# One batch of block-sparse attention written as a list of single steps, with wider block sums, no score bias and fewer unread matmuls

## The chip, the cores and the metric

The kernel runs on one core of one Trainium2 chip. The metric is the device time of one execution in microseconds (us). The span that the profile prints is about 1.8 us shorter than this time, from the first to the last instruction.

## The reference

Four batches of attention, 8 heads, 768 positions, 64 wide. Each query sees the 31 keys nearest to it and one summary per block of 32 keys (the maximum of the keys, the mean of the values). A gated feed-forward layer follows: 3072 tokens, width 512, inner width 1536.

```python
k_sum = k.reshape(B, H, nb, 32, D).max(axis=3)
v_sum = v.reshape(B, H, nb, 32, D).mean(axis=3)
mask_l = np.abs(pos[:, None] - pos[None, :]) < 16
scores_s = scale * einsum('bhsd,bhnd->bhsn', q, k_sum) + np.log(32)
a = softmax(concatenate([where(mask_l, scale * q @ k.T, -1e9), scores_s]))
x = a @ concatenate([v, v_sum])          # per head, then heads side by side
out = (sigmoid(x @ w_gate) * (x @ w_val)) @ w_out
```

## The kernel before

TensorE (PE) is the queue that everything stands in. The heads are taken in four pairs. Batch 0 is special: nothing can hide behind a feed-forward layer that has not begun. So its first half (384 queries) goes through a hand-made list. The second half is spread between the first feed-forward units (a unit is four `gp` and four `vp` matmuls for 128 of the 1536 inner columns), and batches 1 to 3 are spread over the rest. Five pieces matter here.

The keep-busy matmul: it multiplies a tile of ones, and nobody reads the result.

```python
def warm(self, out, n):
    for _ in range(n):
        nc.tensor.matmul(out=out, lhsT=blank, rhs=blank[:, 0:out.shape[-1]], start=True, stop=True)
```

The scores of a pair's first half. The window mask comes in as a matmul that first writes -30720 into the score tile wherever a key is out of reach; the scores are then added on top.

```python
def S1(self, p, step, fill=0):
    if step:
        self.warm(self.fill, fill)
    if step == 0:
        ...
        for i in range(2):
            nc.tensor.matmul(out=self.sc[0:W, i, 0:HALF], lhsT=ident[0:W, 0:W],
                             rhs=bias.rearrange("p t w -> p (t w)"), start=True, stop=False, ...)
        return
    # step 1: 12 small matmuls, start=False; step 2: 2 for the far keys, then exp
```

Block sums of the values, one pair at a time, 26 matmuls of 64 columns in two column groups of the array; and the far part of the weighted sum, 12 matmuls of 64-column weights.

```python
def sums(self, p, fill=0, vsp=None):
    ...
    for t in range(NQ + 1):
        for i in range(2):
            nc.tensor.matmul(out=vsp[64 + 32 * i:96 + 32 * i, 0:64], lhsT=zband[0:64, 30 - 2 * t:62 - 2 * t],
                             rhs=self.vx[0:64, NQ * (2 * p + i) + t, 0:64], ...)

def far(self, p):
    for t in range(6):
        for i in range(2):
            nc.tensor.matmul(out=av[64 * (t % 2):64 * (t % 2) + 64, t // 2, i, 0:64],
                             lhsT=self.P[p][96:120, i, t, :], rhs=vs[96:120, 2 * p + i, :], ...)
```

And the list itself, whose numbers are counts of unread matmuls:

```python
wait(36)
...
a0.T1(0)              # transposes of the keys of pair 0
wait(14)
a0.T2(0, "dve")       # transposes of its queries
a0.S1(0, 0); a0.T1(1); a0.T2(1, "dve"); a0.S1(0, 1); a0.T1(2); a0.S1(0, 2)
a0.S1(1, 0, 6); a0.S1(1, 1); a0.S1(1, 2)
a0.halo(0, 2, 0, 6)
a0.sums(0, 8)
a0.means(0)
a0.near(0)
... # 40 more lines
```

The loads are issued in a fixed order by GpSimd: keys of pairs 1 and 2, values of pair 0, queries of pairs 2 and 3, keys of pair 3, other values, gate weights of units 0 to 3, second half of the queries, the other gate weights.

The softmax here doesn't subtract the row's maximum and nothing guards it: scores larger than these inputs give would overflow.

## Time and profile before

| | before |
|---|---|
| time, median of the first 3 executions | 243.81 us (243.48 to 244.05) |
| span in the profile | 241.5 us |
| PE busy | 234.1 us, 97% of the span |
| unread matmuls | 126 |
| start of the unit after unit 0 of the second half and batch 1's first transposes ("the mark") | 47.26 us |

In the timeline of an engine, a line gives start, duration, engine, source line, operation, output and inputs, shapes, count and, in brackets, the idle time before it and what ended it. Ends on PE are modelled and overlap the next start, so the cost of a step is read from start to start. The lines themselves are in the prediction.

### The profile page before, as it was taken

Reading aid. Unit: us, or ns where it says so; the run is one execution under the profiler, and the core shown is the slowest. Engines: PE = TensorE matmul, PEld = TensorE weight load, DVE = VectorE, ACT = ScalarE, POOL = GpSimd, SP = SyncE. Lnnn points to the kernel's source line nnn. Section 1 sums busy time; section 2 is a strip of 40 time slices with the busy share of each in tenths; the row PEclk is TensorE's granted clock in tenths of the full one; section 3 lists DMA queues with packets and bytes.
Section 4 is the critical chain, followed back from the end, with each engine's and each line's share of the span. In section 5 each row is a group of like instructions: output and inputs, shape, how many; then the busy total and the mean of one; then the engine's idle time right before and its main releaser. Section 6 shows DMA issues by size and latency. Waiting matters only on the chain.

```text
span 241.5 us, 5997 instructions
## 1 busy us (share of the span) xinstructions
PE 234.1 (97%) x2511; PEld 139.5 (58%) x2526; DVE 132.2 (55%) x275; ACT 110.4 (46%) x206; POOL 61.6 (26%) x78
## 2 busy tenths in 40 slices
PE   8999999999999999999999999999999999999993
PEld 7776655666545555556654465566554556665452
DVE  7552799466796318896743057887570043443000
ACT  6654475568861455675311146663211334333121
POOL 8954554435984248800000000000000000000000
PEclk9999999999999999999999999999999999999999
DMA  7999999999999999990028970000045300000222
GB/s 186 165 160 195 203 203 188 134 196 145 137 142 166 172 200 179 140 61 3 0 47 211 205 196 0 3 3 0 1 111 154 131 0 0 1 3 0 87 87 91
DMA packets 85404, 25.99 MB, mean 108 GB/s; under 512 B 71680, under 2 KB 82432, under 8 KB 85376
## 3 DMA queue, kind: packets, MB, share of 16 engines
q0 software_dynamic: 61488, 13.79, 75.1%
q1 hardware_dynamic: 20288, 5.64, 14.3%
q10 hardware_dynamic: 3600, 6.16, 7.7%
q8 instruction: 20, 0.33, 0.6%
q14 instruction: 8, 0.07, 0.1%
HBM read 28.36 MB, written 6.29 MB: 144 GB/s over the span
## 4 chain that ended last, share of the span: by engine, by line
PE 95%; DVE 1%; issue 1%; ACT 1%
PE gp L506 27%; PE vp L506 26%; PE m L542 24%; PE sc L323 3%; PE av L452 2%; PE idle L350 2%; PE tp L207 2%; PE m L527 1%; PE vsp L373 1%; PE br L479 1%; DVE xs L461 1%; PE vsp L350 1%; PE tk L207 1%; PE vsp L357 1%; PE sc L291 1%
## 5 line engine op out<-in xcount | busy, mean ns | idle before, releaser
L514 DVE SCALAR_TENSOR_TENSOR hT<-gate,vp 128x384 bf16<-128x384 f32 x96 | 52.9, 553 | 71.9 <-ACT gate L513 43.8
L506 PE MATMUL gp<-xT,wg 128*128 128x384 bf16 x384 | 79.7, 327 | 0.2
L506 PE MATMUL vp<-xT,wv 128*128 128x384 bf16 x384 | 79.1, 326 | 0.0
L513 ACT ACTIVATE gate<-gp 128x384 f32<-128x384 f32 x96 | 47.1, 492 | 49.8 <-DVE hT L514 33.2
L542 PE MATMUL m<-wo,hT 128*128 128x512 bf16 x261 | 60.3, 379 | 1.4 <-issue 1.0
L506 PEld LDWEIGHTS <-wv 128*128 128x128 bf16 x384 | 37.6, 98 | 24.9 <-issue 0.3
L506 PEld LDWEIGHTS <-wg 128*128 128x128 bf16 x384 | 35.6, 98 | 23.7 <-issue 0.6
L542 PEld LDWEIGHTS <-hT 128*128 128x128 bf16 x276 | 26.2, 98 | 29.7
L547 ACT ACTIVATE ot<-m 128x512 f32<-128x512 f32 x23 | 13.7, 597 | 49.4 <-PE m L542 43.4
L329 ACT ACTIVATE P<-sc 128x768 bf16<-128x768 f32 x28 | 21.4, 811 | 5.4 <-PE sc L323 4.9
L157 POOL DMA_DIRECT2D nat<-in_k_dram x16 | 14.4, 899 | 15.2 <-DMA vx<-in_v_dram 10.4
L163 POOL DMA_DIRECT2D vx<-in_v_dram x18 | 17.2, 982 | 4.0 <-DMA wg<-in_moe_w_gate_dram 2.6
L157 POOL DMA_DIRECT2D nat<-in_q_dram x16 | 13.6, 852 | 10.9 <-DMA vx<-in_v_dram 4.6
L253 DVE TENSOR_REDUCE kTx<-kTn 128x24 bf16<-128x768 bf16 x16 | 15.1, 944 | 0.5 <-ACT kTn L212 0.5
L333 DVE TENSOR_TENSOR P<-P,mask 128x768 bf16<-128x768 bf16 x28 | 14.5, 552 | 0.1
L461 DVE TENSOR_TENSOR xs<-av,rec 128x768 bf16<-128x768 f32 (+1 forms) x16 | 13.7, 858 | 0.6
L393 DVE COPY vx<-vx 32x792 bf16<-32x792 bf16 (+1 forms) x14 | 10.5, 753 | 0.6 <-DMA vx<-in_v_dram 0.3
L350 PEld LDWEIGHTS <-blank 128*128 128x128 bf16 x126 | 8.9, 113 | 2.2 <-DVE blank L599 1.1
L532 DVE TENSOR_SCALAR oe<-m 128x128 f32<-128x128 f32 x2 | 0.6, 292 | 15.0 <-ACT oe L531 15.0
L323 PEld LDWEIGHTS <-kTx 64*128 64x128 bf16 x336 | 5.9, 95 | 4.7 <-issue 3.6
L452 PEld LDWEIGHTS <-P 120*64 120x64 bf16 x336 | 6.1, 111 | 3.5 <-issue 2.4
L323 PE MATMUL sc<-qT,kTx 64*128 64x64 bf16 x336 | 7.8, 191 | 0.0
(92 smaller groups left out, 149.4 us busy)
## 6 DMA issues: line engine op xcount, KB each, us to landing
out_dram<-ot ACTq DMA_DIRECT2D x23, 256.0 KB, 2.4
vx<-in_v_dram POOLq DMA_DIRECT2D x14, 192.0 KB, 8.3
wo<-in_moe_w_out_dram POOLq DMA_DIRECT2D x2, 768.0 KB, 18.0
nat<-in_k_dram POOLq DMA_DIRECT2D x16, 96.0 KB, 7.7
nat<-in_q_dram POOLq DMA_DIRECT2D x16, 96.0 KB, 8.0
nat<-in_q_dram POOLq DMA_DIRECT2D x3, 384.0 KB, 14.0
wg<-in_moe_w_gate_dram POOLq DMA_DIRECT2D x3, 256.0 KB, 9.5
wv<-in_moe_w_val_dram POOLq DMA_DIRECT2D x3, 256.0 KB, 10.1
```

Source lines behind the costliest of these rows:

```text
L157: nc.gpsimd.dma_start(out=nat[:, h // 2, :, 64 * (h % 2):64 * (h % 2) + 64], in_=tap[b, h].rearrange("(c p) d -> p c d", p=128))
L163: nc.gpsimd.dma_start(out=vx_t[b % 2][r0:r1, u0:u1, 0:64], in_=rows_of(v[b, 0, 0:1], (QT * u0 - 16 + r0) * D, [[D, r1 - r0], [QT * D, u1 - ...
L253: nc.vector.tensor_reduce(out=self.kTx[p][:, t, W:KX], in_=self.kTn[p][:, 16:16 + S].rearrange("p (n w) -> p n w", w=32), axis=AX.X, op=AL ...
L323: nc.tensor.matmul(out=sc[:, i, QT * t6:QT * (t6 + 1)], lhsT=kTx[64 * i:64 * i + 64, t, :], rhs=qT[64 * i:64 * i + 64, QT * t:QT * (t + 1) ...
L329: nc.scalar.activation(out=Ph, in_=sc[:, :, 0:6 * QT], func=ACT.Exp, scale=SCALE)
L333: nc.vector.tensor_tensor(out=Ph, in0=Ph, in1=mask[:, None, 6 * hf:6 * hf + 6, :].rearrange("p i t w -> p i (t w)") .to_broadcast([128, 2, ...
L350: nc.tensor.matmul(out=out, lhsT=blank, rhs=blank[:, 0:out.shape[-1]], start=True, stop=True)
L461: nc.vector.tensor_tensor(out=xs[:, 0:3 * G].rearrange("p (g a) i d -> p g (a i) d", g=G), in0=avf[:, :, :, 0:64], in1=rec[:, 0:G].to_broa ...
L506: nc.tensor.matmul(out=o, lhsT=wb[:, c, 128 * f:128 * (f + 1)], rhs=self.xT[:, c, HALF * hf:HALF * (hf + 1)], start=(c == 0), stop=(c == N ...
L513: nc.scalar.activation(out=gate, in_=gp, func=ACT.Tanh, scale=0.5)
L514: nc.vector.scalar_tensor_tensor(out=self.hT[hf][:, f, :], in0=gate, scalar=1.0, in1=vp, op0=ALU.add, op1=ALU.mult)
L542: nc.tensor.matmul(out=self.m3, lhsT=self.hT[hf][:, f, 128 * tt:128 * (tt + 1)], rhs=wo_bf[:, f], start=(f == 0), stop=(f == NF - 1))
```

## The change

The intent is to shorten the stretch before the mark. The hand-made list becomes one text of single steps (transpose, copy, score, exp, mask, ...) in a new order, which goes on until batch 0's second half is done. Two pairs' block sums are done at once, and two tiles' far products at once. The bias matmul is gone; VectorE multiplies the weights by a 0/1 mask after exp, as it did for the later batches. Unread matmuls go from 126 to 41, some of them wider. Three loads move ahead: the queries of pairs 2 and 3 and the keys of pair 3 before the values, and the second half of the queries before the weights of units 2 and 3.

```diff
-    blank = const.tile([128, 128], BF16, name="blank")
+    blank = const.tile([128, 384], BF16, name="blank")
...
-        def S1(self, p, step, fill=0):              # with the bias matmul
+        def n(self, p, fill):                       # near scores, start=True, no bias
+        def f(self, p, fill):                       # far scores
+        def mk(self, p, fill):
+            self.M(p, 0)                            # mask after exp, on VectorE
...
+        def s(self, p, fill):                       # sums of pairs p and p+1
+            for t in range(NQ + 1):
+                for j in range(2):
+                    u = 2 * NQ * (p + j) + t
+                        out=vsp[64 + 32 * j:96 + 32 * j, 0:128], rhs=self.vx[0:64, u:u + NQ + 1:NQ, 0:64],
+        def fa(self, p, fill):                      # far products, two tiles as one weight
+            for a in range(3):
+                for i in range(2):
+                        lhsT=self.P[p][96:120, i, 2 * a:2 * a + 2, :].rearrange("p t w -> p (t w)"),
...
     load_rows(k, 0, 4, 2, 0, S, k0[2])
+    load_rows(q, 0, 4, 4, 0, HALF, q0[:, 0, 4:8])
+    load_rows(k, 0, 6, 2, 0, S, k0[3])
     load_v(0, 1, 25)
     load_v(0, 0, 1, 16, 64)
-    load_rows(q, 0, 4, 4, 0, HALF, q0[:, 0, 4:8])
-    load_rows(k, 0, 6, 2, 0, S, k0[3])
...
     load_gates(0, 2)
+    load_rows(q, 0, 0, H, HALF, HALF, a0.q2)
     load_gates(2, 2)
-    load_rows(q, 0, 0, H, HALF, HALF, a0.q2)
...
-    wait(36)
+    a0.warm(idle[:, 0, 0:256], 13)
...
+    FIRST = """
+        tk0 ck0 tq0:1 tq1 cq0 tk1 ck1 cq1 tk2:8 pk1 n1 ck2 pk2 tq3:3 f1 cq3 tq2 pk0 e1 n0 tk3 cq2 mk1 f0 ck3
+        n2 f2 e0 h0 pk3 e2 n3:12 mk0 f3 e3 h1 s0:2 mk2 ne1 m1 m0 r1 mk3 fa1 ne0 h2 r0 ne2 xs1 fa0 r2 h3 s2:2
+        xs0 ne3 m2 m3 fa2 r3 x0 xs2 fa3 cx0 ... A0 t9 A2 y9 X1 X3 cX1 xb0 w10 cX3 xb2 w11 t10 y10 X2 t11 X0 ..."""
```

A number after a colon is a count of unread matmuls put ahead of that step.

## The prediction

> **What bounds the kernel now.** I read the page first: the busy shares, the slices, the chain that ended last.
>
> ```profile
> span 241.5 us, 5997 instructions
> ...
> PE 234.1 (97%) x2511; PEld 139.5 (58%) x2526; DVE 132.2 (55%) x275; ACT 110.4 (46%) x206; POOL 61.6 (26%) x78
> ...
> PEclk9999999999999999999999999999999999999999
> ...
> PE 95%; DVE 1%; issue 1%; ACT 1%
> ```
>
> The span is a single queue of TensorE work: 97% busy, 95% of the chain, full clock. Waits cannot be what is saved, for there are hardly any. But busy does not mean useful: 126 matmuls on the tile `blank` are read by nobody. So I went to the timeline of PE over the first 48 us (columns: start, duration, instruction, count, idle time before), the only part that the diff touches.
>
> ```profile
> 1.06 3.94 PE L350 MATMUL idle<-blank 128*128 128x128 bf16 x36 [1.06 <-DVE blank L599]
> 4.92 0.53 PE L207 MATMUL tk<-identp,k 128*64 128x128 bf16 x12
> ...
> 13.77 0.84 PE L350 MATMUL vsp<-blank 128*128 128x128 bf16 x12
> 14.54 0.57 PE L357 MATMUL vsp<-vx,zband 64*32 64x64 bf16 x26
> 15.04 0.36 PE L207 MATMUL tq<-identp,nat 128*64 128x128 bf16 x6
> ...
> 16.18 0.49 PE L283 MATMUL sc<-bias,identp 96*96 96x384 bf16 x2
> 16.51 0.33 PE L479 MATMUL br<-identp,xs 128*128 128x128 bf16 x3
> ...
> 44.62 1.27 PE L506 MATMUL gp<-xT,wg 128*128 128x384 bf16 x4
> 45.73 0.81 PE L506 MATMUL vp<-xT,wv 128*128 128x384 bf16 x4
> 46.47 0.86 PE L207 MATMUL tp<-identp,nat 128*64 128x128 bf16 x24
> 47.26 0.82 PE L506 MATMUL gp<-xT,wg 128*128 128x384 bf16 x4
> ```
>
> What a step costs is its start to the next one's start, not its printed duration, since ends overlap. The reader should see unread matmuls, block sums and bias matmuls standing in line with the useful ones. The mark that I use is 47.26: by then unit 0 of batch 0's second half (44.62) and batch 1's first transposes (46.47) are issued. The new kernel does these two in the other order, and from there both kernels have the same list. So the whole difference should be the difference at this mark.
>
> Third, the loads: the timeline of POOL and the issues with their time to landing.
>
> ```profile
> 20.64 0.74 POOL L179 DMA_DIRECT2D wv<-in_moe_w_val_dram  x1 [0.58 <-DMA wg<-in_moe_w_gate_dram]
> ```
>
> This last load of gate weights takes 13.6 us to landing, so 34.2. Issue n waits for issue n-8 to land, so the loads are one stream in list order. Landings so worked out: keys of pairs 1, 2, 3 at 6.0, 7.1, 11.5; values of pairs 0 to 3 at 9.2, 13.6, 15.1, 16.8; gate weights of units 0-1 by 19.0, 2-3 by 21.7; second query half 23.7; units 4-5 by 26.4, 6-8 by 30.3, 9-11 by 34.2.
>
> **What the Trainium skill says.** [...](2) "TensorE: Matmul & The Clock Gate", Part 1: the array starts at half clock and is released after about 3.4 us of activity. The trace agrees: the 36 first unread matmuls start 107 ns apart ((4.92-1.06)/36), later full-array ones 56 ns (six transposes of `br` in 0.33 us). (3) "TensorEngine Tiling (Array Packing)", Key Properties: changing the tiling mode drains TensorE. It agrees: four `vp` matmuls take 0.65 us before `gp` (27.61 to 28.26), but 0.75 before the half-width transposes (28.91 to 29.66). So about 0.1 us per change of shape.
>
> **The change part by part**, TensorE time up to the mark.
> - *Unread matmuls.* After the first 36, twelve groups (90 matmuls) take 5.90 us before, added up start to next start. After: 8 and 12 of 128 columns, 1 and 3 of 320, twice 2 of 384. At 0.056 per 128 columns (so 0.14 and 0.165 for the wide ones) plus one switch a group: 2.56. **-3.34**. The first 36 at half clock become 13 of 256 columns (2.8 us), which end about 4.1. The first transposes need the keys' cast, which ends at 3.89+0.83=4.72 on ScalarE, and start there instead of 4.92: **-0.20**.
> - *No score bias.* Four pairs of bias matmuls (0.45, 0.42, 0.42, 0.33): **-1.62**. It is paid by four masks on VectorE, 0.55 each, between exp and the weighted sums. VectorE is idle over half of 10 to 25 us, so this costs latency, not throughput.
> - *Block sums of two pairs.* Before 4 x 0.50 (one of them has a 0.42 us stall besides). The later batches' form makes four pairs in 0.84 with four column groups, 13 rounds. With two column groups there are still 13 rounds of 128 columns, so about 0.84 for each two pairs: 1.69. Only **-0.3**, and the first must now wait for the values of pair 1 at 13.6.
> - *Far products.* 12 matmuls in 0.31 become 6 with 128-column weights, an estimate of 0.26: **-0.2**.
> - *Order.* Transposes, near products and score steps of one shape now stand together. Fewer switches in these and in the units: about **-0.6**.
> - *Waits and stalls of before that go*: 0.42 in the sums, 0.46 in the unit at 44.62 (which waits for `xT`), 0.26 before unit 2, 0.3 in small ones: **-1.4**.
>
> Sum: 7.7 us less. Against it stand waits that the unread matmuls used to fill. To size them I walked both lists step by step: a step starts when its engine is free, its inputs are done (0.05 us after the end, as the copy of `br` ending 26.02 and unit 0 starting 26.07 show), its PSUM buffer is free (four of one kind, two of the other) and its load has landed, all durations from the rows above. For the old list the walk reaches the mark at 47.3 (trace 47.26). For the new list it reaches it at **42.4**, with these TensorE waits: 0.75 for the first loads; 0.47 for pair 0's key maxima on VectorE; 0.34 for a score buffer (exp of pair 0) and 0.29 for pair 3's maxima; 0.64 for values of pair 2 (15.1, then the halo copy, then near); 0.59 around the copies of `x`; 0.16 at the end. Together **+3.2**. So 7.7-3.2 = 4.5 by parts, 4.8 by the walk. I take 4.6, and the time is 243.8-4.6 = **239.2 us**, -1.9%.
>
> **Rivals.**
> 1. *Unread matmuls were only filling waits.* Then their 3.3 us come back whole, and bias, sums and switches gain perhaps 2.5: 241.3. For it: the timeline of VectorE shows waits of 1.8 us for near products, so the chains are long. Against it: in the new order three or four pairs are in flight at once, and the walk finds 3.2 us of waits in total, not 7.
> 2. *The loads become the bound.* The new list puts the second query half ahead of unit 2's weights: queries at about 21.1, these weights by 23.8. The walk starts Q at 21.1, unit 2 at 23.7, unit 6 at 30.6 (landing 30.3 for `wv`, used at 31.2), unit 9 at 35.0 (34.2, used 35.7). Slack 0.5 to 1.5 us, so nearly bound: the stage cannot end much below 41.5. This caps the gain at about 5.7 us: 238.1.
> 3. *VectorE becomes the bound.* Between 20 and 41 us it has 17 us of work by my list (12 products of 0.47, four masks, four normalisations of 0.7, copies). 80%: it delays single steps, not the sum. If copies into `vx` slow to 0.7-0.9 us as some rows do now (29 to 35 us), up to 1 us is lost.
> 4. *The clock.* In the first 5 us there is now 0.6 us of idle TensorE before 4.72. If the release comes one window later (about 8.2 by the page's 3.4 us), 2.5 us of work doubles, less 0.7 of waits that it fills: +1 to +1.7 us, 240.2 to 240.9. I give it one chance in six.
> 5. *Given back later.* Batch 1 needs its keys and queries (landed by 42.3), values (50.4, first used at 61.1, then 56) and output weights (issue 38.38, landing 56.5, used 66.97, then 62). All keep 4 us or more. For batch 2 the loads and transposes land by about 89, and the first use moves from 91.4 to 86.6, of pair 0, landed by then. I expect nothing to be given back.
>
> **Range and chances.** The walk's error is some 0.5 us either way. The risks (clock, slow VectorE copies, rows that I estimated) lie on the slow side. Range 238.0 to 241.0. Two per cent is 238.93, only 0.3 below my number, so faster by over 2% gets 0.38, within 2% 0.59, slower 0.03.
>
> **What would show it.** Start of batch 1's first transposes near 40.2 and of the second unit (the mark) near 42.4; no `bias` rows; 41 unread matmuls; `vsp` sums of 26 taking 0.84 each with the first at 13.5; far groups near 0.26; PE idle about 4 us in the first 20 (where before shows 0.4 after the start) and nearly none afterwards; everything later shifted by the same amount. I am wrong if the clock record turns full after 5 us, if the gap at the mark differs from the gap at the end by over 0.5 us, if the first-stage waits pass 5 us, or if units 2 to 11 do not stand back to back.

## The result

The changed kernel took 240.51 us in the median of 4 executions (240.46, 240.08, 242.0, 240.57), against 243.69 for the kernel before (4 executions). The ratio is 0.9879, with an interval of 0.9835 to 0.9923: a gain of 1.2%. All ratios here are the mean time of one kernel's fast runs over that of the other's of the same rounds, so not quite the ratio of the medians quoted.

The page of the changed kernel: the span, the busy times, the row of the granted clock and the chain that ended last.

```profile
span 238.7 us, 5652 instructions
...
PE 229.9 (96%) x2342; PEld 134.8 (56%) x2357; DVE 132.9 (56%) x278; ACT 109.8 (46%) x202; POOL 61.1 (26%) x78
...
PEclk9999999999999999999999999999999999999999
...
PE 93%; DVE 2%; ACT 2%; DMA 1%; issue 1%
```

It is still one queue on PE, 2.8 us shorter, and by this page the clock was full throughout. The timeline of PE around the mark shows where the 2.8 us are.

```profile
42.35 0.86 PE L204 MATMUL tp<-identp,nat 128*64 128x128 bf16 x24
43.20 0.81 PE L550 MATMUL gp<-xT,wg 128*128 128x384 bf16 x4
43.84 0.81 PE L550 MATMUL vp<-xT,wv 128*128 128x384 bf16 x4
44.49 0.81 PE L550 MATMUL gp<-xT,wg 128*128 128x384 bf16 x4
```

Here 43.20 is unit 0 and 44.49 is the mark. Before it was 47.26. The difference at the mark is 2.77 us, and the spans differ by 2.8. In the traces of both kernels and of all the experiments below, the stretch from the mark to the end takes 194.18 to 194.22 us (span less mark). So everything was decided before the mark, and nothing was given back later. But the prediction put the mark at 42.4, and 2.1 us of the gain are missing.

The timeline of PE in the first 19 us, where the list was to be quickest:

```profile
1.33 2.95 PE L362 MATMUL idle<-blank 128*128 128x256 bf16 x13 [1.33 <-DVE blank L650]
4.81 0.85 PE L204 MATMUL tk<-identp,k 128*64 128x128 bf16 x12 [0.53 <-ACT k L669]
...
5.97 0.85 PE L204 MATMUL tq<-identp,nat 128*64 128x128 bf16 x12
6.61 0.85 PE L204 MATMUL tk<-identp,k 128*64 128x128 bf16 x12
...
11.71 0.53 PE L204 MATMUL tk<-identp,k 128*64 128x128 bf16 x12
...
15.76 0.90 PE L371 MATMUL vsp<-vx,zband 64*32 64x128 bf16 x26
...
18.41 0.34 PE L437 MATMUL av<-vs,P 24*128 24x64 bf16 x6
```

Twelve transposes of one form take 0.85 us at 4.81, 5.97 and 6.61, and 0.53 us at 11.71. In the kernel before they take 0.53 from the very first (4.92). The transposes come in pairs that start within 6 ns of each other. From one pair to the next it is 101 to 106 ns in the group at 4.81 (once 246), and 52 to 53 later. The same matmuls at half the rate: PE ran at half clock. The trace's own record of the granted clock, which the page sums up only by slices, agrees. Its first entry, "full", comes at **4.77 us** in the kernel before and at **10.23 us** in the changed one. What lies ahead of the first entry is counted as full by the page, so in this trace the clock row prints 9s from the start and the mean clock reads 1.000.

That made the late clock the first theory. The rival was that the walk had been too hopeful about the chains of exp, copies and loads, so that the mark would be near 44 at full clock too, with longer waits in place of slower matmuls.

### The profile page after: what moved, and what is told of

Read it like the earlier page. It is cut to its first block, busy times and chain, and to the rows that moved or that the text cites. A ratio compares the mean times of both kernels' runs of the same rounds, so it can differ in the third digit from the quotient of the medians.

```text
span 238.7 us, 5652 instructions
## 1 busy us (share of the span) xinstructions
PE 229.9 (96%) x2342; PEld 134.8 (56%) x2357; DVE 132.9 (56%) x278; ACT 109.8 (46%) x202; POOL 61.1 (26%) x78
## 3 DMA queue, kind: packets, MB, share of 16 engines
q10 hardware_dynamic: 3600, 6.16, 7.3%
## 4 chain that ended last, share of the span: by engine, by line
PE 93%; DVE 2%; ACT 2%; DMA 1%; issue 1%
PE gp L550 27%; PE vp L550 26%; PE m L593 24%; PE sc L333 3%; PE av L490 2%; PE tp L204 2%; DMA vm<-in_k_dram 1%; PE m L578 1%; PE vsp L388 1%; PE br L517 1%; PE tk L204 1%; DVE xs L502 1%; PE vsp L371 1%; ACT P L305 1%; DVE xs L446 0%
## 5 line engine op out<-in xcount | busy, mean ns | idle before, releaser
L557 ACT ACTIVATE gate<-gp 128x384 f32<-128x384 f32 x96 | 47.3, 493 | 50.5 <-DVE hT L560 35.6
L305 ACT ACTIVATE P<-sc 128x768 bf16<-128x768 f32 x32 | 24.5, 813 | 6.8 <-PE sc L333 5.3
L154 POOL DMA_DIRECT2D nat<-in_k_dram x16 | 13.8, 860 | 12.5 <-DMA vx<-in_v_dram 8.0
L344 DVE TENSOR_TENSOR P<-P,mask 128x768 bf16<-128x768 bf16 x32 | 16.7, 551 | 0.5 <-ACT P L305 0.2
L411 DVE COPY vx<-vx 32x792 bf16<-32x792 bf16 (+1 forms) x14 | 9.4, 673 | 0.4
L522 ACT COPY xT<-br 128x384 bf16<-128x384 bf16 (+1 forms) x12 | 6.6, 589 | 2.9 <-PE br L517 2.0
```

The costliest lines, as they stand in the source:

```text
L154: nc.gpsimd.dma_start(out=nat[:, h // 2, :, 64 * (h % 2):64 * (h % 2) + 64], in_=tap[b, h].rearrange("(c p) d -> p c d", p=128))
L305: nc.scalar.activation(out=self.P[p][:, :, 6 * hf:6 * hf + 6, :].rearrange("p i t w -> p i (t w)"), in_=self.sc[p][:, :, 0:HALF], func=ACT ...
L344: nc.vector.tensor_tensor(out=Ph, in0=Ph, in1=mask[:, None, 6 * hf:6 * hf + 6, :].rearrange("p i t w -> p i (t w)") .to_broadcast([128, 2, ...
L557: nc.scalar.activation(out=gate, in_=self.open[f, hf][0], func=ACT.Tanh, scale=0.5)
```

## The experiments

Eleven runs were made on three chips, eight of them with an edit and three of the changed kernel again; the record has no run e7 or e10. Runs of one call share a chip and the executions of the kernel before: e1 to e4; e5, e6, e8 and e9; e11, a1 and a2. All results were correct. An execution is labelled slow when it is over 1.5% above the fastest of the same kernel; on this one core that is always one in which the mean clock was lower too, but the lower clock also occurs in executions labelled fast. This table gives the clock record of each trace (us from the start of the span). The last column is the time of the execution that was traced.

| trace | turned full | fell to half | full again | mark | time |
|---|---|---|---|---|---|
| before | 4.77 | | | 47.26 | 243.33 |
| after | 10.23 | | | 44.49 | 240.46 |
| e4, the same kernel | 9.88 | | | 44.34 | 240.31 |
| a1, the same kernel | 9.29 | 19.52 | 26.35 | 47.13 | 243.09 |
| a2, the same kernel | 5.24 | | | 42.76 | 238.74 |
| e1 | 6.87 | | | 43.24 | 239.22 |
| e11 | 6.78 | | | 43.64 | 239.61 |
| e8 | 5.51 | | | 43.72 | 239.69 |
| e3 | 4.48 | 14.72 | 24.96 | 46.08 | 242.05 |
| e9 | 5.41 | 12.23 | 29.30 | 49.78 | 245.75 |
| e2 | 6.16 | | | 48.75 | 244.73 |
| e5 | 5.89 | 12.71 | 19.54 | 50.03 | 246.26 |
| e6 | 6.79 | 20.45 | 27.27 | 49.03 | 245.00 |

A fall within the last 2 us of a span is left out (before, e1, e2, e3, e6 and e8 have one). It lowers the mean clock a little (0.996 in e1) and costs nothing that shows: the stretch after the mark is as long in these traces as in the others.

Within a trace all entries of the record lie whole multiples of 3.41 us apart (6.83, 10.24, 17.07). Where the first falls differs from one execution to the next.

### The changed kernel again: e4, a1, a2

No edit. Each was to show how the changed kernel behaves from one execution to the next, and the last two were to catch an early and a late release in the trace.

> The changed kernel unchanged, on the same chip as e1 and e3, for a second record of when the clock is released and for the ratio. Theory 'late clock': again not before 8 us, time 240.1 to 240.7; if the release comes near 5 us in this record, the time of that execution must be near 238.8, otherwise the theory falls.

Measured: 240.31, 241.74, 243.16, 242.87, 240.15, 240.4 (median 241.07), ratio 0.9872 (0.982 to 0.9925), so the result repeats on another chip. Three of the six had a mean clock of 0.986 and were the slower ones.

> The changed kernel once more, one look, to catch an execution with a mean granted clock of 0.986 (4 of its 10 so far, 1.3 to 2.8 us longer). Theory: 0.986 is one fall to half clock for two windows of 3.41 us (6.8/2/240 = 0.014), somewhere in the first 25 us, in executions whose first release came early. If the look has clock 1.0, it must show a first release at 8 us or later and a time of 240.0 to 240.6.

> As a1_look: with clock 0.986, a fall for 6.8 us in the first 25 us and a time of 241.7 to 243.2; with clock 1.0, a first release at 8 us or later and 240.0 to 240.6.

The first (a1) took 243.09 us at a mean clock of 0.986. The second (a2) took **238.74** at 1.000. Both are single executions, so their state is unknown by rule; the clock records tell more than the label. Part of what was expected missed. A look at clock 1.0 was to show a release at 8 us or later and 240.0 to 240.6 us; a2 did neither. A fall was expected where the release came early; in a1 it followed a late one. But what e4's expectation asked of an early release, a time near 238.8, is what a2 has. The timeline of PE in a2, at the start and at the mark:

```profile
4.76 0.74 PE L204 MATMUL tk<-identp,k 128*64 128x128 bf16 x12 [0.48 <-ACT k L669]
...
5.67 0.53 PE L204 MATMUL tq<-identp,nat 128*64 128x128 bf16 x12
...
40.62 0.86 PE L204 MATMUL tp<-identp,nat 128*64 128x128 bf16 x24
...
42.76 0.81 PE L550 MATMUL gp<-xT,wg 128*128 128x384 bf16 x4
```

The transposes speed up within the first group, and the mark is at 42.76; the walk had said 42.4, and 40.2 for the transposes that stand at 40.62. The instructions are the same as in the trace above, whose mark is 44.49. So the chains were judged about right and the rival theory falls. Between these two executions the late release costs 1.73 us at the mark and 1.72 in the time.

In a1 the clock fell later on. Its timeline of PE, for the second group of block sums:

```profile
19.24 1.35 PE L371 MATMUL vsp<-vx,zband 64*32 64x128 bf16 x26
```

The same 26 matmuls took 0.90 in the two groups of the first trace. The fall came at 19.52, within this group, and lasted 6.83 us.

Over the 12 executions of the unchanged changed kernel (4, 6 and 2): one at 238.74 with the early release; six at 240.08 to 240.57 with a mean clock of 1.000 (both that were traced had a late release, at 10.23 and 9.88); five at 241.74 to 243.16 with a mean clock of 0.986 (the one that was traced had a late release and a fall).

### e1: four more unread matmuls at the start

```diff
-    a0.warm(idle[:, 0, 0:256], 13)
+    a0.warm(idle[:, 0, 0:256], 17)
```

> The changed kernel with 17 instead of 13 unread matmuls of 256 columns ahead of the first transposes (3.6 us at half clock instead of 2.8), so that TensorE has no gap before the keys arrive at 4.8. Theory 'late clock': in the changed kernel's trace the first transposes start 101 to 106 ns apart until 10.2 us, where before they start 53 apart from 4.9 on; the gap of 0.7 us kept the clock at half for 5.4 us more. Without the gap full clock comes near 4.8 to 5; the second unit's start (44.49 in the changed kernel, 42.4 in my walk) falls to 42.4-42.9 and the time to 238.3-239.0. Rival 'waits': the stage is held by loads and chains of waits whatever the clock; then the time stays within 0.5 us of the changed kernel, 240.0 or more.

Measured: 239.06 us in the median of six (238.79 to 239.46), ratio 0.9776 (0.9738 to 0.9813). On the same chip the changed kernel without the edit had 241.07. The timeline of PE in e1:

```profile
1.33 3.81 PE L362 MATMUL idle<-blank 128*128 128x256 bf16 x17 [1.33 <-DVE blank L650]
5.06 0.85 PE L204 MATMUL tk<-identp,k 128*64 128x128 bf16 x12
...
6.86 0.51 PE L204 MATMUL tk<-identp,k 128*64 128x128 bf16 x12
```

The transposes start 0.25 us *later* than in the changed kernel, yet the median is 2.0 us lower. Some of this comes from falls, which three of e4's six executions had: against its other three (240.15 to 240.40) e1 is about 1.2 us quicker, and the marks say 1.1 to 1.25. None of e1's six had a fall in mid-list, by their mean clocks, but nothing shows that the four matmuls prevent it. The release was expected near 5 us and the mark at 42.4 to 42.9; they came at 6.87 and 43.24. Four matmuls that nobody reads still pay for themselves several times over. This is the quickest median, below both kernels.

### e11: the same, but behind the gap

Does the clock want an unbroken run of work, or an amount of it? Here the gap at 4.1 to 4.8 stays and four more unread matmuls follow the first transposes.

```diff
-        tk0 ck0 tq0:1 tq1 cq0 ...
+        tk0 ck0 tq0:5 tq1 cq0 ...
```

> The changed kernel with its 13 first unread matmuls, so with the gap of 0.7 us before the keys, but 5 instead of 1 unread matmuls of 320 columns between the key and query transposes of pair 0 (1.07 us more of full-array work at half clock, behind the gap). Theory 'amount': what releases the clock is how much full-array work a window of 3.4 us holds; the release comes at or before 8 us and the time is 239.3 to 240.0, faster than the changed kernel although work was added. Theory 'gap': any gap of 0.7 us spoils the window; release at 9 us or later, time 241.0 to 241.7. In e2_before13 a window with the same gap (0.88 busy) did release the clock, in the changed kernel windows with 0.84 and 0.85 did not.

Measured: 239.61, 238.93, 239.58 and one execution at 244.01 (clock 0.986, labelled slow); ratio 0.9775 (0.9679 to 0.9871) over the three fast ones. The timeline of PE in e11:

```profile
4.77 0.85 PE L204 MATMUL tk<-identp,k 128*64 128x128 bf16 x12 [0.49 <-ACT k L669]
5.56 1.44 PE L362 MATMUL tq<-blank 128*128 128x320 bf16 x5
6.92 0.53 PE L204 MATMUL tq<-identp,nat 128*64 128x128 bf16 x12
```

The release came at 6.78, with the gap within the 3.41 us before it. So an unbroken run is not needed; a2, released at 5.24 with its gap at 4.28 to 4.76, says the same. With work added, the three fast executions were quicker than the six of the changed kernel at 240.08 to 240.57. Four executions, one of them with a fall, are few: I take it for support of the amount, not as a measure of it.

### e3: e1 without the other unread matmuls

```diff
-        tk0 ck0 tq0:1 tq1 cq0 tk1 ck1 cq1 tk2:8 ... tq3:3 ... n3:12 ... s0:2 ... s2:2
+        tk0 ck0 tq0 tq1 cq0 tk1 ck1 cq1 tk2 ... tq3 ... n3 ... s0 ... s2
```

> As e1_warm17, and all the other unread matmuls (1, 8, 3, 12, 2, 2) are taken out of the list. My walk: they stand in waits, so the second unit starts within 0.1 us of e1_warm17 and the time is the same within 0.3. Rival 'they cost their 2.6 us': 2 us or more faster than e1. Rival 'they hold the clock': without them TensorE idles near 5.8 us of the first 20 in pieces of up to 0.7, and the clock falls or comes later: 1 us or more slower than e1, and the starts of matmuls lie 100 ns apart somewhere after 5 us.

Measured: 242.06 (241.16 to 244.35), mean clocks 0.963 to 0.979 in every execution, ratio 0.9908 (0.9861 to 0.9955). It has 28 unread matmuls fewer to run than e1 and is 3.0 us slower. The table of windows for PE (window, its length, busy time with count, granted clock, DMA share, GB/s):

```profile
11.30:14.70 3.40, 1.79 (x48) 1.00 4.96 99
14.70:20.00 5.30, 4.85 (x98) 0.50 2.14 169
20.00:25.00 5.00, 5.00 (x46) 0.50 1.47 197
25.00:30.00 5.00, 5.00 (x51) 1.00 1.35 201
```

PE was busy for 1.79 of 3.40 us, in pieces; its longest idle stretch in the first 20 us after the start was 0.94 us. Then 10.2 us of useful work ran at half rate. So the unread matmuls in the middle of the list hold the clock. The walk had expected the same time as e1 within 0.3 us, so that they only fill waits; this missed.

### e2: the short start in the kernel before

```diff
-    blank = const.tile([128, 128], BF16, name="blank")
+    blank = const.tile([128, 384], BF16, name="blank")
...
-    wait(36)
+    a0.warm(idle[:, 0, 0:256], 13)
```

> The kernel before with only its first unread matmuls shortened to the changed kernel's: 13 of 256 columns instead of 36 of 128. Theory 'late clock': the clock is full only near 8 to 10 us, the dense TensorE work between 4.9 and there takes double, the whole kernel is 1.7 to 2.6 us slower: 245.4 to 246.3. Rival 'waits' (the early list waits for loads anyway, so a slow clock is hidden): within 0.4 us of before.

Measured: 245.83 in the median (243.22 to 249.92, two of six labelled slow), ratio 1.0016 (0.9949 to 1.0084) over the four fast ones. That is inconclusive, and a poor test: the old list has 14 more full unread matmuls right behind the first keys, and the clock of the traced execution was full at 6.16, not near 8 to 10. The mark of the traced execution was 1.49 us later than before; about 0.9 of this is a longer stall that the profile calls "issue" (1.31 us at 20.99, where the kernel before has 0.42 at 18.88), and the rest is about half of the 1.39 us by which the release came later. The spread grew from 3.1 us (eleven executions of the kernel before on this chip) to 6.7.

### e5: the kernel before without the score bias

```diff
-                for i in range(2):
-                    nc.tensor.matmul(out=self.sc[0:W, i, 0:HALF], lhsT=ident[0:W, 0:W], rhs=bias..., stop=False, ...)
...
-                        start=False, stop=True, skip_group_check=True)
+                        start=True, stop=True, skip_group_check=True)
...
+            self.M(p, 0)      # after exp
```

> The kernel before, in its own order, with the bias matmuls taken out and a mask on VectorE after each exp of the first half (this part of the change alone). Theory 'removed work is refilled by the mask's latency': my walk of the old list puts the mark (47.26) only 0.2 us earlier, because near products of pairs 0 and 1 then wait 0.8 and 0.4 us for mask and halo copy on VectorE, and transposes for keys: time 243.3 to 244.0 against 243.8, ratio 0.996 to 1.001. Rival 'TensorE time counts' (the -1.62 of my prediction): ratio 0.993 or lower.

Measured: 245.16 (244.24 to 247.48), ratio 1.0037 (0.9993 to 1.0082). In the old order the removal gains nothing; even the two executions at a mean clock of 1.0 took 245.29 and 244.24. The traced execution had a fall (12.71 to 19.54) and this wait on PE (engine and line, what it waited for, total, times, longest), given with its place in the timeline:

```profile
PE av L397 <- DVE vx L386: 1.2, 1, 1.2
```

```profile
12.51 0.42 PE L397 MATMUL av<-vx,P 120*64 120x65 bf16 x12 [1.22 <-DVE vx L386]
```

The near products wait for the halo copy, which in the old order stands on VectorE behind two of the new masks (10.22 and 11.12, the copy at 11.71; before, the copy started at 9.44). The wait ended at 12.51, before the fall at 12.71 and with the clock full since 5.89. So the fall did not make it; it may have helped to bring the fall, as PE was busy for 0.60 of the 3.41 us before.

### e6: the kernel before without its 76 other unread matmuls

```diff
-    a0.S1(1, 0, 6)
+    a0.S1(1, 0)
-    a0.sums(0, 8)
+    a0.sums(0)
... # and so on; the first 36 and the 14 behind the first keys stay
```

> The kernel before without its 76 unread matmuls after the first 50. Theory 'they cost time in the old order as far as the clock holds': by the walk the mark comes 2.3 us earlier (4.7 us removed, waits for values, gate weights and the copies of x take 2.4): 241.5. Theory 'they hold the clock': with 4 to 5 us of idle TensorE in small pieces between 10 and 27 us the clock falls to half for some 10 us, as in e3_warm17_nofill, and gives back 2 us or more: 243.5 to 246, with the mean granted clock of its executions near 0.98. Rival 'they only fill waits': same time, clock 0.997 or more.

Measured: 244.26 in the median, mean clocks 0.972 to 1.0, ratio 0.9949 (0.9895 to 1.0002) over the four fast ones. The one execution with a clock of 1.0 took 241.31; the others took 243.58 to 245.0. The waits and the windows of PE in the traced one (slow):

```profile
PE vp L506 <- DMA wv<-in_moe_w_val_dram: 2.1, 1, 2.1
```

```profile
17.00:20.40 3.40, 1.57 (x38) 1.00 1.47 196
20.40:27.20 6.80, 6.42 (x67) 0.50 1.44 198
```

With the unread matmuls gone, PE ran ahead of the weights, waited 2.1 us for them, was busy for 1.57 of 3.40 us, and the clock fell. In this list, too, the unread matmuls hold the clock. Where it held by itself, in one execution of six, some 2.5 us were gained.

### e8: e1 with the bias matmuls put back

```diff
+            for i in range(2):
+                nc.tensor.matmul(out=sc[0:W, i, 0:HALF], lhsT=ident[0:W, 0:W], rhs=bias..., start=True, stop=False, ...)
...
         def mk(self, p, fill):
-            self.M(p, 0)
+            pass
```

> e1_warm17 with the score bias put back (its 8 matmuls in the new order) and the four masks taken out: this part alone undone. My sum has 1.62 us for it, the walk with the mask's latency has 0.5: second unit at 43.7 instead of 43.2, time 239.6 against 239.06, ratio to before 0.979 to 0.981. Rival 'TensorE time counts': 240.6, ratio 0.984. Rival 'the mask on VectorE costs more than it saves': not slower than e1.

Measured: 239.97 (239.69 to 240.43, all clocks 0.997 or more), ratio 0.9813 (0.9782 to 0.9844). It ran on another chip than e1, so the ratios to the kernel before are compared: 0.9813 less 0.9776 is 0.9 us of 244. The intervals overlap. The traced marks say the same: 43.72 against 43.24, though e8's clock was full 1.4 us sooner. In the new order the removal is worth about 0.9 us.

### e9: e1 with the loads in their old order

```diff
-    load_rows(q, 0, 4, 4, 0, HALF, q0[:, 0, 4:8])
-    load_rows(k, 0, 6, 2, 0, S, k0[3])
     load_v(0, 1, 25)
     load_v(0, 0, 1, 16, 64)
+    load_rows(q, 0, 4, 4, 0, HALF, q0[:, 0, 4:8])
+    load_rows(k, 0, 6, 2, 0, S, k0[3])
... # and the second half of the queries behind load_gates(2, 2) again
```

> e1_warm17 with the loads issued in the order of before (values of pair 0 ahead of queries of pairs 2 and 3 and keys of pair 3; second query half after the weights of units 2 and 3). By the walk the transposes of queries 3 wait 1.5 us for their load and Q about 0.5: second unit at 45.0 instead of 43.2, time 240.9, ratio 0.985; the idle stretch near 9 to 10.5 us may also make the clock fall or come later, then 242. Rival 'the stage is bound by TensorE work or by later loads': within 0.5 us of e1.

Measured: five fast executions at 241.25 to 242.16, three slow at 245.75 to 246.62 (mean clock 0.965), ratio 0.9876 (0.9837 to 0.9915) over the fast ones. By the ratios the old load order costs 0.0100 of 244, so 2.4 us (on another chip than e1, but the intervals do not overlap). The five had no fall in mid-list, as their mean clocks of 0.996 to 1.0 suggest; whether some had a late release, a mean clock cannot show. The waits of PE in the traced execution, a slow one:

```profile
PE tq L204 <- DMA nat<-in_q_dram: 1.3, 1, 1.3
```

The transposes of pair 3's queries stand early in the new list, and their load came behind the values. In this execution the clock then fell at 12.23 for 17 us.

### What the clock goes by

From the starts and ends of PE's instructions (the ends are modelled, so a hundredth is not to be leaned on) I worked out its busy share in the 3.41 us ahead of each point at which the record could have changed. Early windows that did not bring the release had 0.84, 0.85 and 0.84; those that did had 0.86 (a2, e11), 0.88 (e2) and 0.92 or more. Windows that ended in a fall had 0.45 to 0.77. But 0.61 (e3, right after its release) and 0.66 (e2) did not bring a fall, and after a fall windows of 0.87 to 1.00 did not bring the release at once. It took two to five of them. So busy share goes with it but is not the whole rule. What exactly is measured stays open.

An earlier release could also be luck, if the windows merely fell differently. Three traces rule this out for e1 and e11. Counted in steps of 3.41 us, the changed kernel's record could have turned full at 6.82 (10.23 less one step) and did not. That of e11 did at 6.78 and that of e1 at 6.87. With the windows in the same place within 0.1 us, the added matmuls brought the release one window earlier. In a2 the place itself differed: its window ended at 5.24, with 0.86 busy. These are single traces.

## Why the prediction was right or wrong

The time and its range held: 239.2 said, 240.51 measured, range 238.0 to 241.0, and within 2% was the likeliest of the three. Part of this is luck: the median of the six in e4 was 241.07, just outside, and the prediction's own sign of being wrong came (a clock record that turns full after 5 us). The gain was 3.2 us, not 4.6, and one step is the main reason: the release of the clock.

- **The mark decides: right.** The gap at the mark and at the end agree within 0.1 us, and rival 5 (given back later) came out as it was told.
- **The walk: right for what it assumed.** At an early release (a2) the mark was at 42.76 and the time 238.74. PE was idle for 3.2 us of the first 20 there (20 less 16.81 busy), where about 4 had been expected. In a2 the mark is 4.50 us earlier than before, where the sum by parts had 4.5. This is partly luck too, as two of the parts were overstated (below), so other terms must have erred the other way.
- **The clock: the step that failed.** The prediction counted the shorter warm-up as a gain of 0.20 ("end about 4.1 ... start there instead of 4.92"), and gave the late release, its rival 4, "one chance in six". It came in three of the four traces of the changed kernel. Eleven of twelve executions were slower than the early-release one by 1.3 to 4.4 us. The size was well told: 240.2 to 240.9 for a late release, against 240.08 to 240.57, though the release came at 9.29 to 10.23 and not at about 8.2. What was misjudged is how sure a release is. The Trainium skill ("TensorE: Matmul & The Clock Gate", Part 1) says that the window runs freely and that the same kernel can be released sooner or later; these traces agree, with first releases at 5.24 to 10.23 us in one kernel. The work of the first 3.5 us has a hole of 0.53 us that ends at 4.81, and the unread matmuls ahead of it last less than a window (2.95 us). So every 3.41 us window that ends before 8.2 holds some idle time; with 17 matmuls (e1), one that begins at 1.33 or later holds none. Why idle time counts is argued from the timelines, and a2 and e11 were released with the hole in their window; that e1 and e11 turn full a window earlier is measured.
- **A fall in mid-list was on no list.** Five of twelve executions had a mean clock of 0.986 and took 241.74 to 243.16; the one of them that was traced (a1) shows the fall. This is why the median of the repeat was 241.07.
- **Unread matmuls, -3.34: half the story, and too large.** By the prediction's own 0.1 us a switch, the six groups left cost 2.34+0.6 = 2.94 us, not 2.56; in a2 they take 2.93 from start to next start. So the term was -2.97. And they do two jobs, filling waits and holding the clock. Taking them out of the old list gained some 2.5 us in the one execution whose clock held, and nearly nothing otherwise (e6). Taking the last of them out of the new one cost 3.0 us (e3). Rival 1 put both jobs down to the first.
- **Small slips.** The prediction says that waits cannot be what is saved, and then counts 1.4 us of waits and stalls that go. It reads "full clock" from the row, although the record turns full only at 4.77. And 47.3 less 42.4 is 4.9, not 4.8.
- **Score bias, -1.62: mis-sized.** Alone in the old order it gained nothing (e5). In the new order it gained about 0.9 (e8), by ratios from two chips whose intervals overlap, with the traced marks on the same side.
- **Sums and far products: right.** The two sums groups take 0.83 each from start to start (15.76 to 16.59, 19.11 to 19.94; 0.84 said), the far groups 0.26 to 0.28 (0.26 said).
- **Load order: not given a value of its own.** Measured at 2.4 us (e9), it is worth more in the new order than the score bias, the other part that was undone alone there. Rival 2 watched whether the loads would bind in the new order; it did not ask what the old order would have cost.

## What to carry to other kernels

A matmul that nobody reads may be holding the clock: before removing one, look in the record of the granted clock, or at the duration of equal matmuls early and late, for where the rate changes, and keep every 3.4 us of the stretch in which waits stand (here the first 20 us) well filled. Where a list sits near such an edge, run it a dozen times, for a single trace shows one outcome out of three. And value parts in the order in which they will run: taking out the bias gained nothing in the old list and about 0.9 us in the new one. What the loads' new order would be worth in the old list was not tried.

## What the Trainium skill lacked or had wrong

- "TensorE: Matmul & The Clock Gate", Part 1, says that the ramp penalty is below 1% of a typical span and advises not to fit a specific count of slow matmuls. In 239 us, a late release cost 1.7 us (0.7%, so within that), but this was more than a third of the gain at stake (4.6 us), and executions with a fall took up to 4.4 us (1.8%) more than the one with the early release.
- The same page's table at the end gives "No PE-idle gaps >~3µs" as the rule against falls. Here the clock fell where the longest gap of the 3.41 us before was 0.81 us (e3: busy for 1.79 of 3.40 us, then 10.2 us at half rate). Its section "A second HAM failure mode: psum-queue depth-cycling" does name frequent micro-idles, and agrees, but gives no share: here windows with 0.45 to 0.77 fell, and two with 0.61 and 0.66 did not.
- The same page gives one busy window of about 3.4 us for the release, without saying how busy. At the start, windows with 0.84 to 0.85 did not do it and 0.86 did; after a fall it took 6.8 to 17.1 us, though PE was busy for 0.87 to 1.00 of each window.
- No page says that a mean granted clock can hide the start: the changed kernel's reads 1.000 while its matmuls ran at half rate until 10.23 us (0.85 against 0.53 us for twelve equal transposes).
- "TensorEngine Tiling (Array Packing)", Key Properties, says that a change of tiling mode drains TensorE, without a figure. Here a change of shape costs about 0.1 us: four `vp` matmuls take 0.65 us before more of their kind and 0.75 before half-width transposes, and the six groups of unread matmuls in a2 take 2.93 us where their columns alone make 2.34. That this is a drain is not shown.
